# Moving a batch's key products from the first transform into the first feed-forward layer

## The chip, the cores and the metric

The kernel runs on one core of a Trainium2 chip. The metric is the device time of one execution in microseconds (us); lower is better. A core has a matrix engine (TensorE, PE in the profile, with its weight loads as PEld), VectorE (DVE), ScalarE (ACT), GpSimd (POOL), and SyncE (SP), which here issues nearly all DMAs.

## The reference, cut to what matters

Eight batches of 576 tokens, eight heads of 64 (so 512 columns), all float32. Attention of the "efficient" kind comes first, then a Fourier mix, a normalisation and two layers:

```
q_s = softmax(q over the 64 of a head)        k_s = softmax(k over the 576 tokens)
kv  = k_s^T v    (64x64 for each head)        x   = q_s kv            -> (batch, 576, 512)
u   = x + real(fft over tokens and columns of x)
un  = (u - mean) / sqrt(var + 1e-6)           (per token)
out = u + relu(un @ w1) @ w2                  (512 -> 2048 -> 512)
```

## The kernel before, in words

**Tiling.** Of each batch's 576 tokens, 512 are its own rows (four tiles of 128: `xpart(b, c, u)`), and the other 64 of two batches are gathered in a shared tile. So there are eight groups of 512 rows for the own tokens, and a ninth group (`B` = 8) for the shared ones. `attention(b)` runs stages over items: four key items (`k_load`, `k_exp`, `k_turn`, `k_times_v`: load two heads' keys and values, exponential, five transposes, ten recorded passes of matmul into `kvr`), and four query items (`q_load` to `q_times_kv`). `transform(b)` folds the tokens, runs five `block(k)` steps on PE and evacuates them on ACT into `Z` and `ZT`; `mix_own` and `mix_shared` (through `second`) finish the Fourier mix and add it to x. `norm(g)` takes the statistics, normalises and transposes x into `unT`.

**The order.** Group 0 goes through the layers plainly (`plain`): 16 `up(f)` steps of 128x512 matmuls with a relu on ACT, then 64 `part(i, f)` steps (`DOWN`). All later groups use Strassen's seven products (`up`, `down`). While PE is in group 0's layers, the other engines bring the weights into shape: `fetch(i)` loads one of 32 raw blocks of 512 KB, `convert(i)` makes floats of them (two activations on ACT, two operations on DVE, one on POOL), and `combine(layer, p)` forms the sums that Strassen needs and stores them in DRAM (`w1s`, `w2s`), from where later groups stream them. `WORDS_AT` says in which place each raw block lies; a place is used again when its block is converted (`after`). Side steps of batch 1 (attention, transform, mix, norm) are put between the 64 `part` steps by the list `gaps`.

**What sets the order.** The program's order is a priority: Tile's scheduler may let a ready instruction of later code run in a gap of its own planned time, on each engine's in-order queue. So the code has one-element operations that make later work wait: `wait_for(t, raws)` holds blocks of weights until t is there, `gate(t, raw)` does the same for other data, and `hold()` keeps the tiles q, k and v from being loaded before a given relu `f` of `up` is done (`free(f)`).

**What the change touches.** In the kernel before, batch 1's four key items are loaded at the start (`first`, lines 225 to 252, into spare space), their maxima and exponentials run in `second_keys` (lines 441 to 465) beside the folds of the first transform, and their transposes and products run as `products` between batch 0's mix and `norm(0)`:

```
one, two = front(0)
keys, products = blk.second_keys()
for step in one + keys + two + products + norm(0):
    step()
```

Eighteen conversions are in the program's 16 `up` steps (after the first four), and ten are left for the `part` steps.

Of the kernel before, what the change touches and what calls it, by code (L numbers as in the profile page):

```python
# [40 lines left out]
F32 = mybir.dt.float32  # L41
I32, U32 = mybir.dt.int32, mybir.dt.uint32
ACT = mybir.ActivationFunctionType
# [30 lines left out]

WORDS_AT = [*range(8), 8, 9, 10, *range(3, 8), 0, 1, 2, 8, 9, 10, 4, 5, 6, 7, 8, 9, 10, 11, 12, 13]
ORDER = (1, 6, 5, 7, 2, 4, 3)
# [46 lines left out]
class _Block:  # L123
    def __init__(self, ctx, tc, q, kT, v, w1, w2, ft, cd, out):
# [50 lines left out]
        self.xs, self.live, self.stream = {}, {}, {}  # L175
        self.turns = 0
        self.unused = None

# [31 lines left out]
    def first(self, fetch):  # L210

        nc, b = self.nc, 0
        at = 2 * NF * D

        def place(n):
            nonlocal at
            at += n
            return self.big[:, at - n:at]

        ks = [place(S) for _ in range(NR)]  # L220
        v = place(NC * D).rearrange("p (c n) -> p c n", n=D)
        own = [place(2 * D).rearrange("p (c n) -> p c n", n=D) for _ in range(2)]
        tail = place(D)

        k1 = self.spare(NR * S)
        flat = self.w1sb[:, NF - 2:, :].rearrange("p a n -> p (a n)")
        v1 = [self.spare(NC * P), self.spare(NC * P), place(NC * P), flat[:, 0:NC * P]]
        self.unused = None
        self.second_at = k1, [t.rearrange("p (c n) -> p c n", n=P) for t in v1]
# [17 lines left out]
        for r in range(NR):  # L247
            cols = slice(r * P, (r + 1) * P)
            t = self.second_at[1][r]
# [56 lines left out]
    def weights(self):  # L306
# [6 lines left out]
        def fetch(i):  # L313

            at = WORDS_AT[i]
            if at < 8:
                raw = self.w2sb[:, 2 * at:2 * at + 2, :].rearrange("p a n -> p (a n)")
            elif at < 11:
                raw = self.words[at - 8][:].rearrange("p a n -> p (a n)")
            else:  # L320
                raw = self.spare(2 * D)
# [95 lines left out]
    def attention(self, b, loads=None):  # L417
# [22 lines left out]

    def second_keys(self):


        nc, V = self.nc, self.nc.vector
        items = [("k", 1, r) for r in range(NR)]
        m, rec = (self.small.tile([P, NR], F32, tag=n, name=n, bufs=1) for n in ("km1", "krec1"))

        def maxima():
            self.gate(self.at_start[2][0][:, 1, :], self.second_at[0][0:1, ::S])
            for it in items:  # L450
                self.k_load(it)
                V.reduce_max(m[:, it[2]:it[2] + 1], self.live[it][0], axis=AX.X, negate=True)
            self.gate(self.xpart(0, 1, 1), m[0:1, :])

        def exps():
            for it in items:
                k, i = self.live[it][0], slice(it[2], it[2] + 1)
                nc.scalar.activation(k, k, ACT.Exp, bias=m[:, i], accum_out=rec[:, i])
                self.live[it].append(rec[:, i])

            t = self.small.tile([P, 1], F32, tag="root", name="root", bufs=1)
            nc.scalar.activation(t[:], rec[:, NR - 1:], ACT.Sqrt)
            V.tensor_scalar(out=rec[:], in0=rec[:], scalar1=ATT_EPS, scalar2=None, op0=ALU.add)
            V.reciprocal(rec[:], rec[:])
        return [maxima, exps], pipelined(items, [self.k_turn, self.k_times_v])

    def gate(self, t, raw):

        n = int(np.prod(raw.shape))
        raw, one = raw.bitcast(I32), t.bitcast(I32)[0:1, 0:n]  # L470
        if len(raw.shape) == 3:
            one = one.rearrange("p (a b) -> p a b", b=raw.shape[2])
        self.nc.vector.scalar_tensor_tensor(out=raw, in0=one, scalar=0, in1=raw, op0=ALU.bitwise_and,
                                            op1=ALU.bitwise_or)

    def k_load(self, it):
        nc, (_, b, r) = self.nc, it
        if b == 0:
            ks, v = self.at_start[:2]
            self.live[it] = [ks[r], v[:, :, r * P:(r + 1) * P]]  # L480
            return
        if b == 1:
            self.live[it] = [self.second_at[0][:, r * S:(r + 1) * S], self.second_at[1][r]]
            return
        k = self.work.tile([P, S], F32, tag="k", name="k", bufs=2)[:]
        v = self.work.tile([P, NC, P], F32, tag="v", name="v", bufs=2)
        nc.sync.dma_start(k, self.kT[b, r * P:(r + 1) * P, :])
# [24 lines left out]
    def k_turn(self, it):  # L512
# [3 lines left out]
        for c in range(4):  # L516
            nc.tensor.transpose(pt[:, c, :], k[:, c * P:(c + 1) * P], self.ident[:])
        nc.scalar.copy(ks[:, 0:4, :], pt[:])
        pt = self.turned()

# [5 lines left out]
    def k_times_v(self, it):  # L526
# [5 lines left out]
        for h in range(2):  # L532
            s = slice(64 * h, 64 * h + 64)
            to = self.kvr[b % 2][s, r, s]
            if b == 1:

                nc.scalar.mul(to, pk[s, s], rec[s, 0:1])
            else:
                nc.vector.tensor_scalar(out=to, in0=pk[s, s], scalar1=rec[s, 0:1], scalar2=None, op0=ALU.mult)

    def q_load(self, it):
# [8 lines left out]
        self.nc.sync.dma_start(q, self.q[b, tokens(c, u), :])  # L550
        self.live[it] = [q]

    def t_load(self, it):
# [85 lines left out]
    def transform(self, b):  # L639
# [36 lines left out]
        def at_first():  # L676
# [4 lines left out]

            self.wait_for(eo[1][:, NN:], [self.raws[0]])

# [34 lines left out]
    def second(self, z, zr, add):  # L718
# [13 lines left out]
        nc.scalar.copy(paired(sn[:, 0:HD]), interleaved(pm[:, HD:]))  # L732
        if self.turns == 1:

            self.gate(sn[:], self.second_at[0][0:1, ::S])
        two = self.halves()
# [16 lines left out]
    def mix_own(self, b, c):  # L753
# [3 lines left out]
        def add(lo, hi):  # L757
            for u, (f, g) in enumerate(((lo, hi), (hi, lo))):
                x = self.xpart(b, c, u)
                self.added(x, f, g)  # L760

        self.second(lambda k: Z[:, k, s], self.Zr[:, s], add)

    def norm(self, g):
# [22 lines left out]
        def normal(i):  # L787
            un = self.halves()
            x = self.xpart(g, i % 2, i // 2)
            if g == 0:  # L790
                V.tensor_scalar(out=un[:, 0:D], in0=x, scalar1=std[:, i:i + 1], scalar2=mv[:, i, 0:1], op0=ALU.mult,
                                op1=ALU.add)
                if i == 0:
                    words = self.w2sb.rearrange("p f n -> p (f n)").rearrange("p (a n) -> p a n", n=2 * D)
                    self.gate(un[:], words[0:1, 1:4, 0:2])
                if i == 1:
# [205 lines left out]
def kernel(ctx: ExitStack, tc: tile.TileContext, q, kT, v, w1, w2, ft,  # L1002
# [52 lines left out]
    one, two = front(0)  # L1055
    keys, products = blk.second_keys()
    for step in one + keys + two + products + norm(0):
        step()

    groups = [*range(B - 1), B, B - 1]  # L1060
    for order, g in enumerate(groups):
        loads = [] if g == 0 else None
        one, two = front(order + 1, loads) if order + 1 < B else (blk.later, [])
        if g == 0:
            up, down = blk.plain(0, nexts.pop(0))

            round_blocks(range(4))
            n = 2 * NF - 14
            for f in range(NF):
# [7 lines left out]
            for step in loads:  # L1077
                step()
            for i in range(3):
                fetch(2 * NF - 3 + i)  # L1080

            side = one + two + norm(1)
            gaps = [6] + [4] * (len(one) - 1) + [3] * 5 + [1] * 4 + [2] * (len(two) - 9) + [1] * 7
            at = 0
            for i in range(len(down)):
                down[i]()
                for step in rest[i // 3:i // 3 + 1] if i % 3 == 0 else []:
                    step()
                for step in combine[i * len(combine) // 60:(i + 1) * len(combine) // 60]:
                    step()  # L1090
# [63 lines left out]
```

## Time and profile before

| | |
|---|---|
| median of 3 runs | 1135.42 us (1135.22, 1135.42, 1136.85) |
| the profiled execution | 1136.85 us, span in the trace 1135.1 us |
| busy share of the span | PE 97%, PEld 81%, DVE 47%, ACT 36%, POOL 29% |
| mean granted TensorE clock | 0.993 |
| DMA | 193.79 MB, mean 171 GB/s |
| first `up` matmul of group 0 | 65.56 us from the span's start |
| first `part` matmul of group 0 | 122.15 us |
| first matmul of the next group's layers | 202.25 us |

Views of the trace give busy time per engine, and for the idle time before an instruction what ended it (the releaser). "Timeline" lines have: start in us, duration in us, engine (a trailing q is the engine's queue), source line, operation, output<-input, shape, count, and in brackets the idle time before with its releaser. "Waits" lines have: engine, tile and line of the waiting instruction, the releaser, total us, times, longest us. "Windows" lines have the stretch, its length, and for each engine busy us and the number of instructions, then the granted TensorE clock, the mean busy share of the DMA engines and GB/s.

### The profile page before, as it was taken

The page shows a single profiled execution, that of the slowest core. Times are in us where ns is not written, and L with a number is a line of the kernel's source. Part 1 is how long each engine was busy: PE and PEld are TensorE (multiplying, and loading weights), DVE is VectorE, ACT ScalarE, POOL GpSimd, SP SyncE. Part 2 cuts the span into 40 slices and gives each one's busy share as a digit, 9 for nine tenths or more (in the row PEclk, how much of TensorE's full clock was granted, in tenths as well). Part 3 has the DMA queues.
Part 4 walks back from the last instruction along what each step waited for, and adds up shares of the span by engine and source line. Part 5 has one row for each costly group of instructions (what it writes and reads, how often), then busy time and mean ns, then how long its engine had stood idle before and what let it go on. Part 6 is the DMA issues. An engine that isn't in the chain of part 4 may idle for free.

```text
span 1135.1 us, 14578 instructions
## 1 busy us (share of the span) xinstructions
PE 1096.6 (97%) x5448; PEld 916.9 (81%) x5448; DVE 533.4 (47%) x1094; ACT 404.6 (36%) x975; POOL 332.2 (29%) x304
## 2 busy tenths in 40 slices
PE   5789999999999999999999999999999999999997
PEld 4644455888888988888889888888889888888886
DVE  6675756368434724384344733592434352203201
ACT  6595523355233513371325322451334152201200
POOL 2055462235003610334024402260034213402320
PEclk9899999999999999999999999999999999999999
DMA  9557675555346534544356425552453344444451
GB/s 312 166 190 227 244 272 161 169 208 167 113 156 215 182 140 144 194 158 177 122 178 220 149 103 183 190 198 107 144 191 150 113 154 160 175 150 151 156 185 55
DMA packets 92549, 193.79 MB, mean 171 GB/s; under 512 B 23088, under 2 KB 59696, under 8 KB 85312
## 3 DMA queue, kind: packets, MB, share of 16 engines
q1 hardware_dynamic: 90680, 191.82, 49.6%
q10 hardware_dynamic: 1800, 1.05, 0.3%
q8 instruction: 43, 0.70, 0.2%
q14 instruction: 26, 0.21, 0.1%
HBM read 168.72 MB, written 28.31 MB: 174 GB/s over the span
## 4 chain that ended last, share of the span: by engine, by line
PE 83%; DVE 4%; DMA 3%; ACT 2%; issue 2%; POOL 1%; SPq 0%; POOLq 0%; ACTq 0%; DVEq 0%
PE bb L905 15%; PE bb L943 15%; PE bc L943 10%; PE ba L943 10%; PE bc L905 10%; PE ba L905 9%; PE acc L531 3%; PE acc L613 2%; PE acc L725 1%; PE acc L701 1%; PE acc L704 1%; DMA w2s<-big 1%; PE bc L844 1%; PE tr L805 1%; PE tr L581 1%
## 5 line engine op out<-in xcount | busy, mean ns | idle before, releaser
L905 PE MATMUL bb<-unT,big 128*128 128x256 f32 x768 | 187.8, 381 | 0.3 <-DVE u L873 0.3
L943 PE MATMUL bb<-big 128*128 128x256 f32 x768 | 172.1, 379 | 0.0
L943 PEld LDWEIGHTS bb<-big 128*128 128x128 f32 x768 | 145.4, 190 | 20.3
L905 PEld LDWEIGHTS bb<-unT,big 128*128 128x128 f32 x768 | 142.8, 190 | 23.5 <-DVE u L873 3.1
L354 POOL TENSOR_TENSOR big<-big 128x512 f32<-128x512 f32 (+1 forms) x38 | 46.4, 1220 | 281.4 <-ACT big L917 273.9
L905 PE MATMUL bc<-unT,big 128*128 128x256 f32 x512 | 125.6, 379 | 0.0
L905 PE MATMUL ba<-unT,big 128*128 128x256 f32 x512 | 123.6, 379 | 0.0
L917 ACT ACTIVATE big<-big 128x512 f32<-128x512 f32 x96 | 60.3, 628 | 173.8 <-DVE big L916 173.5
L943 PE MATMUL bc<-big 128*128 128x256 f32 x512 | 116.0, 379 | 0.5 <-DVE x L960 0.5
L877 DVE TENSOR_TENSOR u<-bb,s 128x512 f32<-128x512 f32 x40 | 27.6, 691 | 186.1 <-PE bb L943 128.3
L943 PE MATMUL ba<-big 128*128 128x256 f32 x512 | 114.8, 379 | 0.0
L943 PEld LDWEIGHTS bc<-big 128*128 128x128 f32 x512 | 96.1, 190 | 14.3 <-DVE x L960 0.9
L943 PEld LDWEIGHTS ba<-big 128*128 128x128 f32 x512 | 95.6, 190 | 12.1
L905 PEld LDWEIGHTS bc<-unT,big 128*128 128x128 f32 x512 | 95.1, 190 | 12.6
L905 PEld LDWEIGHTS ba<-unT,big 128*128 128x128 f32 x512 | 95.0, 190 | 11.8
L362 POOL TENSOR_TENSOR unT<-unT 128x512 f32<-128x512 f32 x8 | 14.2, 1774 | 182.9 <-DVE unT L361 182.9
L570 ACT ACTIVATE q<-q,qm 128x64 f32<-128x64 f32 x240 | 62.1, 339 | 13.8 <-DVE qm L568 13.8
L873 DVE TENSOR_TENSOR u<-bb,s 128x512 f32<-128x512 f32 x40 | 27.6, 690 | 74.3 <-PE bb L905 35.2
L955 POOL TENSOR_TENSOR x<-x,u 128x512 f32<-128x512 f32 x14 | 17.7, 1267 | 147.8 <-DVE u L877 111.2
L916 DVE TENSOR_TENSOR big<-bc,u 128x512 f32<-128x512 f32 x64 | 44.1, 689 | 25.3 <-PE bc L905 24.5
L869 ACT COPY s<-ba 128x512 f32<-128x512 f32 x40 | 23.4, 586 | 88.6 <-PE ba L905 45.5
L809 ACT COPY unT<-tr 128x512 f32<-128x512 f32 x36 | 20.7, 585 | 78.8 <-PE tr L805 78.4
(230 smaller groups left out, 1647.3 us busy)
## 6 DMA issues: line engine op xcount, KB each, us to landing
big<-w1s SPq DMA_DIRECT2D x64, 896.0 KB
big<-w2s SPq DMA_DIRECT2D x56, 1024.0 KB
big<-in_w_dram SPq DMA_DIRECT2D x20, 512.0 KB
q<-in_q_dram SPq DMA_DIRECT2D x27, 256.0 KB
k<-in_kT_dram SPq DMA_DIRECT2D x24, 288.0 KB
v<-in_v_dram SPq DMA_DIRECT2D x24, 256.0 KB
words<-in_w_dram SPq DMA_DIRECT2D x9, 512.0 KB
w2s<-big SPq DMA_DIRECT2D x8, 512.0 KB
```

What stands on the lines that cost most here:

```text
L354: e1.tensor_tensor(out=to(4), in0=at(2), in1=at(3), op=ALU.add)
L531: nc.tensor.matmul(pk, lhsT=ks[:, c, :], rhs=v[:, c, :], start=(c == 0), stop=(c == NC - 1))
L570: nc.scalar.activation(heads[:, h, :], heads[:, h, :], ACT.Exp, bias=m[:, h:h + 1])
L613: nc.tensor.matmul(px[:, r * P:(r + 1) * P], lhsT=qT[:, r, :], rhs=self.kvr[b % 2][:, r, :], start=True, stop=True)
L809: nc.scalar.copy(unT[:, u:u + 3:2, :, cols], pt[:].rearrange("p (a k) t -> p a k t", a=2))
L869: nc.scalar.copy(temp("s1"), box["ba"][:])
L873: V.tensor_tensor(out=temp("u2"), in0=box["bb"][:], in1=box["s1"][:], op=ALU.add)
L877: V.tensor_tensor(out=temp("u3"), in0=box["bb"][:], in1=box["s1"][:], op=ALU.add)
L905: nc.tensor.matmul(bank()[:, i, :], lhsT=w[:, WA_AT[m], k * P:(k + 1) * P], rhs=unT[:, B_AT[m], k, :], start=first and i == 0 and k == 0, ...
L916: V.tensor_tensor(out=hp(i), in0=bank[:], in1=u[:], op=ALU.add)
L917: nc.scalar.activation(hp(i), hp(i), ACT.Relu)
L943: nc.tensor.matmul(bank()[:, i, :], lhsT=h[p][:, A_AT[m], i * P:(i + 1) * P], rhs=w[:, p, :], start=first and i == 0 and p == 0, stop=p == ...
```

## The change

Batch 1's key items are no longer done at the start. They go back into `attention(1)` as the first four items, loaded and computed between the `part` steps of group 0. Their loads go into two k and v tiles held until relu 12, and into spare space (the place of `unT`, which is free when the last `up` step is done). In the place of the removed steps come: three junk matmuls (`warm`) behind each of the four x updates of batch 0's mix; a root that loads ACT's table at the end of the first folds; a looser hold on the weights, so that four blocks instead of one may be converted during the first transform's blocks. Twenty-four instead of eighteen conversions stand in the `up` steps, and four instead of ten among the `part` steps; the last three raw blocks get places 7, 8, 9 instead of three spare ones. The products of batch 1 are scaled by DVE instead of ACT, and batch 1's query exponentials wait for its third key's transposes (`held_back`).

```diff
-WORDS_AT = [..., 4, 5, 6, 7, 8, 9, 10, 11, 12, 13]
+WORDS_AT = [..., 4, 5, 6, 7, 8, 9, 10, 7, 8, 9]
...
-        k1 = self.spare(NR * S)
-        flat = self.w1sb[:, NF - 2:, :].rearrange("p a n -> p (a n)")
-        v1 = [self.spare(NC * P), self.spare(NC * P), place(NC * P), flat[:, 0:NC * P]]
...
-            load(self.second_at[0][:, r * S:(r + 1) * S], self.kT[1, cols, :])
-            load(t[:, 0:4, :], self.v[1, 0:512, cols].rearrange("(c p) n -> p c n", p=P))
-            load(t[:, 4, :], self.v[1, S - P:, cols])
...
-        held = {12: [("q", D, 3)] * 3, 15: [("k", S, 2)] * 2 + [("v", NC * P, 2)] * 2}
+        held = {12: [("k", S, 2)] * 2, 14: [("q", D, 3)] * 3}
...
-        if b == 1:
-            items = []
...
-    def second_keys(self):
...
-    def gate(self, t, raw):
...
+        if b == 1 and r > 1:
+            k, v = self.spare(S), self.spare(NC * P).rearrange("p (c n) -> p c n", n=P)
...
+        if it[1:] == (1, 2):
+            self.wait_for(ks[:, 0, :], [q.bitcast(I32) for q in self.held_back])
...
-            if b == 1:
-                nc.scalar.mul(to, pk[s, s], rec[s, 0:1])
-            else:
-                nc.vector.tensor_scalar(out=to, in0=pk[s, s], scalar1=rec[s, 0:1], ...)
+            nc.vector.tensor_scalar(out=self.kvr[b % 2][s, r, s], in0=pk[s, s], scalar1=rec[s, 0:1], ...)
...
-            self.wait_for(eo[1][:, NN:], [self.raws[0]])
+            t = self.small.tile([P, 1], F32, tag="root", name="root", bufs=1)
+            V.tensor_scalar(out=t[:], in0=eo[1][:, NN:NN + 1], scalar1=0.0, scalar2=None, op0=ALU.mult)
+            nc.scalar.activation(t[:], t[:], ACT.Sqrt)
+            self.wait_for(eo[1][:, NN:], [self.raws[i] for i in range(4)])
...
                 self.added(x, f, g)
+                if b == 0:
+                    self.warm(x[:, 0:HD], 3)
...
-    for step in one + keys + two + products + norm(0):
+    for step in one + two + norm(0):
...
-            n = 2 * NF - 14
+            n = 2 * NF - 8
...
-            for i in range(3):
-                fetch(2 * NF - 3 + i)
...
-            gaps = [6] + [4] * (len(one) - 1) + [3] * 5 + [1] * 4 + [2] * (len(two) - 9) + [1] * 7
+            gaps = [2] + [2] * 4 + [8] + [2] * (len(one) - 6) + [3] * 5 + [1] * 4 + [2] * (len(two) - 9) + [1] * 7
+            other = rest + combine
...
-                for step in rest[i // 3:i // 3 + 1] if i % 3 == 0 else []:
-                    step()
-                for step in combine[i * len(combine) // 60:(i + 1) * len(combine) // 60]:
+                for step in other[i * len(other) // 60:(i + 1) * len(other) // 60]:
```

More of the change, by code (lines that the diff above doesn't have):

```diff
@@ L72 @@
 WB_AT = {1: 0, 2: 1, 3: 2, 4: 6, 5: 4, 6: 5, 7: 3}
-WORDS_AT = [*range(8), 8, 9, 10, *range(3, 8), 0, 1, 2, 8, 9, 10, 4, 5, 6, 7, 8, 9, 10, 11, 12, 13]
+WORDS_AT = [*range(8), 8, 9, 10, *range(3, 8), 0, 1, 2, 8, 9, 10, 4, 5, 6, 7, 8, 9, 10, 7, 8, 9]
 ORDER = (1, 6, 5, 7, 2, 4, 3)
@@ L176, in __init__ @@
         self.turns = 0
+        self.held_back = []
         self.unused = None
@@ L223, in first @@
         tail = place(D)
-        k1 = self.spare(NR * S)
-        flat = self.w1sb[:, NF - 2:, :].rearrange("p a n -> p (a n)")
-        v1 = [self.spare(NC * P), self.spare(NC * P), place(NC * P), flat[:, 0:NC * P]]
-        self.unused = None
-        self.second_at = k1, [t.rearrange("p (c n) -> p c n", n=P) for t in v1]
         load = nc.sync.dma_start
@@ L246, in first @@
         self.tables()
-        for r in range(NR):
-            cols = slice(r * P, (r + 1) * P)
-            t = self.second_at[1][r]
-            load(self.second_at[0][:, r * S:(r + 1) * S], self.kT[1, cols, :])
-            load(t[:, 0:4, :], self.v[1, 0:512, cols].rearrange("(c p) n -> p c n", p=P))
-            load(t[:, 4, :], self.v[1, S - P:, cols])
         for i in range(11):
@@ L317, in fetch @@
                 raw = self.w2sb[:, 2 * at:2 * at + 2, :].rearrange("p a n -> p (a n)")
-            elif at < 11:
+            else:
                 raw = self.words[at - 8][:].rearrange("p a n -> p (a n)")
-            else:
-                raw = self.spare(2 * D)
             raw = raw.bitcast(I32)
@@ L439, in attention @@
         return steps
-    def second_keys(self):
[L444 to L465, printed above, removed]
-    def gate(self, t, raw):
[L469 to L474, printed above, removed]
     def k_load(self, it):
@@ L481, in k_load @@
             return
-        if b == 1:
[L483 to L486, printed above, removed]
+        if b == 1 and r > 1:
+            k, v = self.spare(S), self.spare(NC * P).rearrange("p (c n) -> p c n", n=P)
+        else:
+            k = self.work.tile([P, S], F32, tag="k", name="k", bufs=2)[:]
+            v = self.work.tile([P, NC, P], F32, tag="v", name="v", bufs=2)
         nc.sync.dma_start(k, self.kT[b, r * P:(r + 1) * P, :])
@@ L533, in k_times_v @@
             s = slice(64 * h, 64 * h + 64)
[L534 to L539, printed above, removed]
+            nc.vector.tensor_scalar(out=self.kvr[b % 2][s, r, s], in0=pk[s, s], scalar1=rec[s, 0:1], scalar2=None,
+                                    op0=ALU.mult)
     def q_load(self, it):
@@ L551, in q_load @@
         self.live[it] = [q]
+        if b == 1:
+            self.held_back.append(q)
     def t_load(self, it):
@@ L732, in second @@
         nc.scalar.copy(paired(sn[:, 0:HD]), interleaved(pm[:, HD:]))
-        if self.turns == 1:
-            self.gate(sn[:], self.second_at[0][0:1, ::S])
         two = self.halves()
@@ L792, in normal @@
                                 op1=ALU.add)
-                if i == 0:
-                    words = self.w2sb.rearrange("p f n -> p (f n)").rearrange("p (a n) -> p a n", n=2 * D)
-                    self.gate(un[:], words[0:1, 1:4, 0:2])
                 if i == 1:
@@ L1055 @@
     one, two = front(0)
-    keys, products = blk.second_keys()
-    for step in one + keys + two + products + norm(0):
+    for step in one + two + norm(0):
         step()
```

## The prediction

> **What bounds the kernel now.** I read the page first (busy shares, slices), then the waits of PE, then timelines of the two places where PE is not full.
>
> ```profile
> PE 1096.6 (97%) x5448; PEld 916.9 (81%) x5448; DVE 533.4 (47%) x1094; ACT 404.6 (36%) x975; POOL 332.2 (29%) x304
> PE   5789999999999999999999999999999999999997
> PEclk9899999999999999999999999999999999999999
> ```
>
> PE is the bound from the third slice (57 us) on. The slices before it have spare PE time, and the change takes work out of there and puts it where PE is full. How full is told by the waits of PE between the first `up` matmul of group 0 (65.56 us) and the first matmul of the next group (202.25 us):
>
> ```profile
> PE acc L701 <- ACT ZT L712: 2.7, 1, 2.7
> PE tr L805 <- ACT eo L799: 1.5, 2, 0.9
> PE ba L835 <- ACT unT L809: 1.1, 1, 1.1
> PE acc L613 <- ACT qT L588: 0.9, 1, 0.9
> ```
>
> That is 6.2 us of waits in 136.7 us, so whatever PE work is added there costs nearly its length. Now the stretch before it, timeline from 50 us, where the key products (L517, L521, L531, L537) stand between batch 0's mix and its norm:
>
> ```profile
> 52.01 1.28 DVE L774 BATCH_NORM_STATS2 st<-x 128x6 f32<-128x512 f32 x2
> 53.42 1.27 DVE L774 BATCH_NORM_STATS2 st<-x 128x6 f32<-128x512 f32 x2
> 55.83 0.63 ACT L537 ACTIVATE kvr<-acc,krec 64x64 f32<-64x64 f32 x2 [1.47 <-PE acc L531]
> 57.38 0.30 ACT L778 ACTIVATE std<-mv,eps 128x2 f32<-128x2 f32 x1
> 57.71 0.17 DVE L779 RECIPROCAL std<-std 128x2 f32<-128x2 f32 x1 [3.02 <-ACT std L778]
> 59.28 1.00 DVE L791 TENSOR_SCALAR eo<-x,std,mv 128x512 f32<-128x512 f32 x2
> 59.84 1.38 PE L531 MATMUL acc<-big,ks 128*128 128x128 f32 x10 [0.79 <-ACT ks L518]
> 61.05 1.04 PE L805 MATMUL tr<-ident,eo 128*128 128x128 f32 x8
> 62.66 1.08 ACT L809 COPY unT<-tr 128x512 f32<-128x512 f32 x2
> ```
>
> The first statistics are done at 53.5, but the root (L778) comes at 57.38, because ACT's queue holds the key copies and scalings that wait for PE; DVE idles 3.02 us for it. The normalised x is done at 60.28, and its transposes then stand behind the fourth key product on PE. So the key products delay the first `up` step here.
>
> **The change part by part.** *Start of group 0's layers.* Without the products the root runs right behind the first pair of statistics (53.5 + 0.3), and the reciprocal behind the second pair, which ends at 54.7 and 0.2 later with its aggregate: 54.9 instead of 57.71, or 2.8 earlier. From the reciprocal to the last normalised tile before took 60.28 - 57.71 = 2.6, so 57.5. The first transposes need only the first tile (55.7) and no longer wait for a product; copies of 0.59 follow, the last of four transposes at about 57.6 to 58.2, its copy to 58.9, `up` at 59.0: 6.5 earlier. Against it: four conversions may now run during the transform's blocks. Each takes 0.65 + 0.68 on ACT and twice 0.69 on DVE (L342, L347, L343, L344). ACT was busy 2.70 of 5 us in 40 to 45 and 2.17 in 45 to 50, so there is room for the 5.3 us, but one of these operations in front of a Z copy, one in front of an add and one in front of a root cost up to 0.7 each. I take 1.0 in all (bounds 0 and 4): `up` starts 5.5 earlier (2.5 to 6.5). The maxima taken out (L452, 2.73 us at 29.34) saved nothing: they end at 32.07, and the next fold needs an x copy that ends at 32.01. The twelve `warm` matmuls lie behind the x updates and end before the first transposes.
>
> The table of the root was loaded at 37.15 in 1.28 us (L462), in an ACT gap. It can still load there, since the load itself waits for nothing, or beside the blocks; I count 0.3, inside the 1.0. "ScalarE: Activation LUTs", What ACT_TABLE_LOAD costs, in the Trainium skill gives such a switch 2.66 us with a drain behind the load; the row shows the root directly behind its 1.28 us, and with the page's figure beside the blocks the forecast would be some 1.4 us higher.
>
> *The key items on PE.* Batch 2's, run inside Strassen's layers at full clock, show their price (timeline of PE, 210 to 245 us):
>
> ```profile
> 214.41 0.60 PE L517 MATMUL tr<-ident,k 128*128 128x128 f32 x4
> 214.85 0.27 PE L521 MATMUL tr<-ident,k 128*128 128x128 f32 x1
> 217.55 1.28 PE L531 MATMUL acc<-v,ks 128*128 128x128 f32 x10
> ```
>
> By start to next start that is 214.41 to 214.96 = 0.55 and 217.55 to 218.66 = 1.11, so 1.66 for one item, 6.6 for four. All of it now lies among the `part` steps, where PE is full: +6.6.
>
> *Waits of the key items.* `k_exp`, `k_turn`, `k_times_v` now follow each other by two `part` steps, 1.7 us, on PE's in-order queue; what is queued behind a late one is all the rest of the layer. The keys themselves are in time: relu 12 falls at about 60 + 13 x 3.43 + 0.6 = 105, and two keys need 3 us to land; the two in the spare place are issued when `up` ends (some 116.5) and turned about 8 us later. But ACT's ks copy (0.58) and DVE (5.00 of 5 us busy in 125 to 130) must answer within 1.7 us. Bounds: 0, and 3.6 (four times the 0.9 by which PE waited for qT in this stretch). Batch 2's own four keys waited 1.1 once and 1.2 in two, so I take 1.5, nearer to these.
>
> *Loads, conversions, stores.* Keys and values of batch 1 (2.36 MB) go from the start, where they pushed the raw weights back, to 105 to 120 us; the DMA engines were 0.32 busy in 110 to 120, which covers them. They stand on SP in front of the queries, whose exponentials moreover wait (`held_back`, four one-element operations on DVE) for the third key's ks copy, about 125 us; that costs nothing while the first query is turned at step 18, some 137 us, and one query's exponentials take 2.0 us on ACT (L570). Twenty-four conversions in 55 us of `up` need 24 x 1.38 = 33 us of DVE and 32 + 16 x 0.6 = 42 us of ACT: covered. The `part` steps lose six conversions (8.3 us of DVE, 7.7 of POOL) and get the keys (four times 0.74 + 0.30 + 0.58 = 1.6 us of DVE, the scaling among it). Zero; without that cover a conversion behind time would hold a `part` at its own 1.3 us.
>
> *The stall at 180 us.*
>
> ```profile
> 178.93 0.77 ACT L507 ACTIVATE k<-k,km 128x576 f32<-128x576 f32 x1 [4.92 <-DVE km L505]
> 180.28 0.76 PE L701 MATMUL acc<-ft,eo 128*128 128x144 f32 x4 [2.75 <-ACT ZT L712]
> 182.80 1.06 SPq L392 DMA_DIRECT2D w2s<-big  x2
> 180.00:185.00 5.00, 4.72 (x13) 2.66 (x14) 1.92 (x5) 1.64 (x12) 1.63 (x2) 0.66 0.73 224
> ```
>
> Z copies of batch 1 stand on ACT behind an exponential of batch 2's second key, whose load stands on SP behind w2s stores and whose maximum stands on DVE behind the sums of w2. PE waits 2.75 us and then runs at a granted clock of 0.66: 181.67 to 184.77 for four passes of 0.43, some 1.8 us more. I keep this 4.5 us as it is (bounds: gone, or as now).
>
> "TensorE: Matmul & The Clock Gate", Part 1, in the Trainium skill has the clock halved after an idle window of about 3.4 us; here 2.75 us of wait were enough. Taken as a threshold, the rule would price this stall at 2.75 us, and the faster rival would lie 1.8 us nearer to the forecast.
>
> Sum: -5.5 + 6.6 + 1.5 = +2.6. The profiled execution took 1136.85 us (span 1135.1 and 1.75 around it), so 1139.4 against it; but it is the highest of three, and I put the difference on the median, 1135.4: **1138.0**. The first `up` step starts cold in both (granted clock 0.68 in 65.5 to 70), so no difference is taken from that.
>
> **The rivals.** *Faster: the combine chain gets a head start.* `combine` can begin when `up` ends (POOL L354 waited 12.3 us for L279, until 120.03), which is 5.5 us earlier, while batch 1's Z copies stay where they are in time, since the key items fill that gain. If the last w2s stores move from 182.8 to before 177, the key of batch 2 is loaded early and the 4.5 us stall goes, with it the 0.9 us wait for qT; with key waits of 0.5: -5.5 + 6.6 + 0.5 - 5.4 = -3.8, 1131.6. It decides from the point where ACT's Z copies wait under 0.5 us. For it: six conversions less on POOL and DVE behind 120 us. Against it: the w2 sums stand later in the program among the steps than before, and DVE and ACT have the keys first.
>
> *Slower still: the start moves little.* The conversions let loose in the first transform take ACT and DVE in front of the mix, and `up` starts only 2.5 us earlier: -2.5 + 6.6 + 1.5 = +5.6, 1141.0. For it: ACT put a conversion (42.33) in front of the second block's Z copy already before. Against: about 5 of 10 us of ACT are free there.
>
> *No change:* 6.5 us gained, no wait of the keys: +0.1, 1135.5.
>
> **How the numbers follow.** A change of 0.2%, 2.3 us, is about what a measurement of this kernel can tell from none. The forecast has 0.42 (0.30 slower by more than that, 0.12 within); the faster rival 0.29 (0.25 faster, 0.04 within); the small start 0.16, all slower; no change 0.13 (0.08 within, 0.03 faster, 0.02 slower). Faster 0.28, same 0.24, slower 0.48. The forecast's own range is 1135.5 to 1141.6 (start 4 to 6.5 earlier, waits 0 to 3.6). The whole range reaches over the rivals, 1130.1 (the faster one with a start 6.5 earlier and no waits: -5.3) to 1143.1 (start 2.5 earlier, waits 3.6: +7.7), leaving out what lies past these ends and new waits that no row shows.
>
> **What would show it.** Right: the first `up` matmul near 60 us, the root behind its statistics; key pieces of 0.55 and 1.11 us on PE between 117 and 140; the first matmul of the next group 2 to 3 us behind 202.25, and all later groups shifted by the same. Wrong: `up` at 63 or later; PE waits for ks or k above 4 us; no wait of PE for ZT near 180 and a next group that starts before 200; or a difference that arises after the next group has started, which nothing here foresees.

## The result and the profile after

| | before | changed |
|---|---|---|
| median, four runs of each on one chip | 1135.32 us (1134.85 to 1136.85) | 1140.72 us (1138.83 to 1142.04) |
| ratio | | 1.0044, interval 1.0025 to 1.0062 |
| ratio on a second chip (run `after_again`) | 1137.18 us (31 runs, 1131.59 to 1140.68) | 1139.48 us, 1.0025, interval 1.0007 to 1.0043 |
| profiled execution, span | 1136.85 us, 1135.1 | 1142.04 us, 1140.2 |
| first `up` matmul | 65.56 | 60.98 |
| first `part` matmul | 122.15 | 117.5 |
| first matmul of the next group, in the timeline of PE | 202.09 | 202.91 |
| first matmul of `down` in the seventh Strassen group | 982.7 | 987.9 |

By the two ratios the change makes the kernel slower by 2.8 and 5.0 us; the forecast was 2.6. (The start of the next group before is 202.09 us in the timeline; the 202.25 given earlier is in no view.) The page's first lines, its slices and its clock show nothing of how:

```profile
PE 1101.9 (97%) x5472; PEld 922.9 (81%) x5472; DVE 541.6 (47%) x1110; ACT 402.9 (35%) x967; POOL 332.3 (29%) x302
PE   5899899999999999999999999999999999999997
PEclk9999999999999999999999999999999999999999
```

The start of group 0 is where the forecast was made first. Timeline from 50 us:

```profile
52.09 1.28 DVE L727 BATCH_NORM_STATS2 st<-x 128x6 f32<-128x512 f32 x2
53.37 0.66 DVE L330 TENSOR_SCALAR big<-bc 128x512 int32<-128x512 int32 x1
54.15 0.30 ACT L731 ACTIVATE std<-mv,eps 128x2 f32<-128x2 f32 x1 [0.28 <-DVE mv L728]
55.92 0.17 DVE L732 RECIPROCAL std<-std 128x2 f32<-128x2 f32 x1
59.24 0.63 PE L755 MATMUL tr<-ident,eo 128*128 128x128 f32 x4 [0.80 <-DVE big L250]
60.98 2.04 PE L785 MATMUL ba<-unT,big 128*128 128x512 f32 x2 [1.11 <-ACT unT L759]
```

The root (L731) stands 0.28 us behind its statistics, as forecast, and no key product is in front of the transposes. One conversion (L330) was let in between the statistics of the second and third tile, and the second reciprocal came at 55.92 instead of the 54.9 of the working: one of the costs for which 1.0 was set aside.

Now PE's waits from the first `up` matmul to the next group. They hold one new line, and the forecast's four old ones are down to the wait for unT:

```profile
PE acc L484 <- ACT ks L468: 3.8, 1, 3.8
PE ba L785 <- ACT unT L759: 1.1, 1, 1.1
PE tr L755 <- ACT unT L759: 0.2, 1, 0.2
PE acc L564 <- DVE kvr L487: 0.2, 1, 0.2
```

The 3.8 us are explained by the timeline of the other engines in front of 128.09:

```profile
125.07 0.93 DVE L343 TENSOR_TENSOR big<-big 128x256 f32<-128x256 f32 x1 [2.63 <-POOL big L341]
125.92 0.74 DVE L455 TENSOR_REDUCE km<-spare 128x1 f32<-128x576 f32 x1
126.69 0.78 ACT L457 ACTIVATE spare<-spare,km 128x576 f32<-128x576 f32 x1 [8.37 <-DVE km L455]
127.47 0.56 ACT L468 COPY ks<-tr 128x512 f32<-128x512 f32 x1
128.09 1.75 PE L484 MATMUL acc<-v,ks 128*128 128x128 f32 x10 [3.84 <-ACT ks L468]
129.63 1.06 PE L467 MATMUL tr<-ident,k 128*128 128x128 f32 x4
130.69 1.85 PE L794 MATMUL bb<-big 128*128 128x512 f32 x2
```

PE had turned the first key at 121.82. ACT's copy of it (L468) stood in ACT's queue behind the third key's exponential (L457), that one waited for its maximum (L455), and the maximum stood on DVE behind a sum of `combine` (L343) that waited for POOL. So the first key waited for the third, whose load had been issued only at 118.78, and the third waited for sums of weights. That it was the sums and not the load itself is read from the chain that ended last: it goes from a w1s store (118.30, 4.51 us) over POOL's sums (123.63 and 124.36) to the maximum.

The stall at 180 us is gone. First from the kernel before, SP's issue of batch 2's second key with the stores ahead of it, and PE's first step of the transform's blocks:

```profile
170.64 2.42 SPq L392 DMA_DIRECT2D w2s<-big  x2
174.64 0.79 SPq L487 DMA_DIRECT2D k<-in_kT_dram  x1
170.01 0.66 PE L701 MATMUL acc<-ft,eo 128*128 128x144 f32 x4
```

And from the changed kernel, SP's issues of both keys, ACT's first exponential and first Z copy, and the same step of PE:

```profile
164.54 0.44 SPq L437 DMA_DIRECT2D k<-in_kT_dram  x1
166.78 0.37 SPq L437 DMA_DIRECT2D k<-in_kT_dram  x1
175.63 0.78 ACT L457 ACTIVATE k<-k,km 128x576 f32<-128x576 f32 x1 [12.44 <-DVE km L455]
177.52 0.37 ACT L661 COPY Z<-acc 128x256 f32<-128x256 f32 x1
175.29 0.66 PE L655 MATMUL acc<-ft,eo 128*128 128x144 f32 x4
```

Before, the second key's load stood behind two w2s stores and its exponential in front of the Z copies, at 178.93. Now the load is 7.9 us earlier, PE's blocks begin 5.3 us later, and both exponentials are done (at 177.4) when the first Z copy is due. Windows of the changed kernel (PE is full where before had a wait; the other two belong to the ks wait):

```profile
126.00:128.00 2.00, 0.00 (x0) 0.00 (x0) 1.36 (x5) 1.31 (x3) 0.00 (x0) 1.00 1.05 406
130.00:132.00 2.00, 2.00 (x7) 1.37 (x6) 1.92 (x5) 1.23 (x3) 0.68 (x1) 0.50 0.01 5
175.00:185.00 10.00, 10.00 (x44) 6.57 (x43) 6.01 (x14) 4.45 (x19) 4.56 (x6) 1.00 0.68 223
```

Up to the next group the two executions differ by 0.8 us only. The rest of the difference in the profiled run arises later, first in the next group. The chain that ended last (start, length, what):

```profile
248.20 0.64 PE tr L532 x4
248.85 5.63 DMA q<-in_q_dram
...
256.49 1.49 DVE q L526
...
258.01 0.66 PE tr L532 x4
```

A query of batch 2 is loaded when the transposes of another have freed its place (248.84), lands 5.63 us later, and after its normalising PE has waited 2.39 us for it. With the half clock behind this wait (0.66 in 258 to 260, 0.50 in 260 to 262) the distance from the next group's start to the one after it is 126.7 us instead of 123.8. Before, the queries of that batch went to PE at other times, with one wait of 0.94 at 256.29. Another 1.4 us arise two groups on (123.5 us instead of 122.0 from one group's start to the next), where PE waits 2.03 us for a query at 502.28.

### The profile page after: what moved, and what is told of

Same layout as the page of the kernel before. It is cut to its first block, busy times and chain, and to the rows that moved or that the text cites. A ratio compares the mean times of both kernels' runs of the same rounds, so it can differ in the third digit from the quotient of the medians.

```text
span 1140.2 us, 14646 instructions
## 1 busy us (share of the span) xinstructions
PE 1101.9 (97%) x5472; PEld 922.9 (81%) x5472; DVE 541.6 (47%) x1110; ACT 402.9 (35%) x967; POOL 332.3 (29%) x302
## 4 chain that ended last, share of the span: by engine, by line
PE 86%; DVE 5%; DMA 3%; ACT 3%; issue 1%; POOL 1%; SPq 0%; ACTq 0%; POOLq 0%; DVEq 0%
PE bb L893 15%; PE bb L855 14%; PE bc L893 10%; PE ba L893 10%; PE bc L855 10%; PE ba L855 9%; PE acc L484 3%; PE acc L564 2%; PE bc L794 2%; PE acc L655 2%; PE acc L658 2%; PE acc L679 1%; PE tr L532 1%; PE tr L755 1%; PE tr L467 1%
## 5 line engine op out<-in xcount | busy, mean ns | idle before, releaser
L349 POOL TENSOR_TENSOR unT<-unT 128x512 f32<-128x512 f32 x8 | 14.2, 1775 | 183.0 <-DVE unT L348 183.0
L661 ACT COPY Z<-acc 128x256 f32<-128x256 f32 (+1 forms) x32 | 12.0, 375 | 107.1 <-PE acc L658 107.1
```

## The experiments

Each ratio is to the kernel before on the same chip. Two executions of one kernel can differ by more than what is looked for here, so the ratios carry the verdicts, and the profiles the places.

**The two kernels again.** Unaltered.

> The changed kernel once more, unaltered, for a second trace. If the loss of 5 us has the three places that its first trace shows (0.8 us by the start of the next group, 2.9 in that group's up layer, 1.4 in the up layer two groups on), they stand in the second trace as well, each within 0.5 us, and the time is 1138 to 1142. If the two later places are chance of one execution (loads that landed late), they are gone or elsewhere in this trace, and the time is nearer to 1138.

Measured: 1.0025, interval 1.0007 to 1.0043, span 1136.5. The ks wait was there again (3.7 us), the stall at 180 was not, `up` began at 60.8 and the next group at 202.5. The query wait in the next group was half as long, and the clock stayed at 1.00 behind it:

```profile
PE tr L532 <- DVE q L526: 1.2, 1, 1.2
```

From the next group's start to the `down` of the seventh took 785.0 us in the first profile and 781.5 in this one. So 3.5 us of the first profile's loss differ from one execution to the next: 2.1 in the next group, where the wait was half as long and the clock stayed full, and the 1.4 two groups on, which are gone.

> The kernel before, unaltered, for a second trace. Theory: its stall near 180 us (ACT's Z copies behind the second exponential of batch 2) is a matter of the order in ACT's queue, so it is there again, with 2 to 3.5 us of wait and slow clock behind it, and from the first part to the next group it takes 79 to 81 us as in the first trace (79.9). Rival: it came from one late load; then the wait is under 1 us here and the distance is near 75.

Measured: one execution of 1139.1 us, span 1137.3. The stall was there again (3.1 us for ZT, granted clock 0.75 in 175 to 185), so it lies in the order on ACT and not in one execution. First `up` 64.4, next group 203.8 (81.5 us after the first `part`, a little over the 79 to 81 expected), and 780.7 from there to the same `down` (780.6 in the first profile). Against this execution the second one of the change is 3.6 us earlier at `up` and 1.3 earlier at the next group, where the first pair of profiles had 4.6 earlier and 0.8 later. So a term read from one pair of profiles holds to a microsecond or two, no better.

**The third key held.** In `k_exp` of the changed kernel:

```diff
+        if it[1] == 1 and it[2] > 1:
+            self.wait_for(self.kss[it[2] % 2][:, 0, :], [k.bitcast(I32)])
```

> The changed kernel with one wait more: the exponentials of batch 1's third and fourth key wait for the ks copies of the first and second, so that ACT has the copy first; nothing is loaded earlier. Theory A (the loss at 124 us is ACT's order: a copy that was ready stood behind an exponential whose data were not): PE's wait of 3.84 us for ks falls below 1 us, the slow clock behind it goes, and the next group starts 4 to 6 us earlier, at 197 to 199; time some 1135 to 1137. Rival B (the keys' loads are late, whatever the order): the wait only moves to the third key's transposes on PE, and the next group still starts at 202 to 203; time as changed, 1139 to 1141.

Measured: 1.0003, interval 0.9989 to 1.0018. PE's waits between 100 and 200 us:

```profile
PE acc L566 <- DVE kvr L489: 1.6, 1, 1.6
PE bc L787 <- ACT big L789: 1.3, 1, 1.3
PE tr L534 <- DVE qrec L526: 0.8, 1, 0.8
PE acc L486 <- ACT ks L470: 0.6, 2, 0.3
```

The ks wait falls from 3.8 to 0.6 with the clock loss behind it, and the next group starts at 200.3, later than the 197 to 199 expected. It was 202.9. Of the 5.6 us of wait and lost clock (worked out below), 0.6 stay and 2.4 come back as waits for DVE (the last key's scaling and a query's sum). The difference to the unaltered change is 1.0025 - 1.0003 = 0.22%, 2.5 us. The intervals overlap, but the runs of the two, taken together on one chip, hardly do: nine of ten of `order_only` (median 1136.73) are under the lowest of `after_again` (1137.66, median 1139.48). So the order that makes the ks wait is shown to be that part of the loss.

**The third key loaded earlier.** Its keys go into the tile of Z instead of the spare place:

```diff
-            k, v = self.spare(S), ...
+            k = self.spare(S) if r == 3 else self.work.tile([P, KT * HD], F32, tag="Z", ...)[:, 0:S]
```

> The changed kernel with the third key of batch 1 in the idle space of Z, so that its load needn't wait for the end of up; its values and the fourth key stay in the spare space. Theory A (ACT's order): the third key's exponential is done before the first copy, so PE's wait for ks falls below 1 us, as in the other kernel; next group at 197 to 199, time 1135 to 1137. Rival B (loads): the fourth key and the third's values are as late as before, so 2 us or more of PE waits stay between 120 and 145 us, and the time stays above 1138.

Measured: 0.9999, interval 0.9981 to 1.0016. No ks wait is left; the kvr wait of 1.6 and one of 0.9 for qT are. Another way to the same end, and the same time within its interval. The next group starts at 201.75, not at the 197 to 199 expected; behind the waits for qT and kvr the clock halved (see the end).

**The scaling back on ACT.** `order_only`, with batch 1's products scaled by ACT as before the change:

```diff
+            if b == 1:
+                nc.scalar.mul(to, pk[s, s], rec[s, 0:1])
```

> The changed kernel with the wait that puts the ks copies first, and with batch 1's products scaled by ACT as in the kernel before instead of DVE. Theory A (with the order mended, DVE's queue is what is late next: the fourth key's scaling stood behind query work and PE waited 1.6 us for it): that wait goes, the next group starts 1 to 2.5 us before the 200.3 of the version with the order alone, and the time falls to 0.1 to 0.2% below the kernel before. Rival (PE's later steps wait anyway for the queries): a wait of the same size for q or qT takes its place, and the next group starts at 200 to 201.

Measured: 0.9997, interval 0.9983 to 1.0011, the same as `order_only`. The kvr wait went, and in its place came

```profile
PE acc L486 <- ACT ks L470: 2.0, 1, 2.0
```

with the next group at 200.3 again, as the rival said: a wait of the same size took its place, here in front of the second key's product (130.42) instead of the query product that needed the last key's scaling (146.81).

**The stall taken out of the kernel before.** Batch 2's first two key loads wait for its last Z row:

```diff
+        if b == 2 and r < 2:
+            nc.vector.tensor_copy(k[0:1, 0:1], self.Zr[0:1, 0:1])
```

> The kernel before with the loads of batch 2's first two keys held until the last Z copy of batch 1's transform, so that no exponential stands in front of those copies on ACT. Theory A: the stall at 180 us is that order alone; PE's 2.75 us wait for ZT and the half clock behind it go, and the next group starts 4 to 4.5 us earlier, near 198; time 1130.5 to 1132. Rival B: the stall is due to w2's sums and stores on DVE and SP, which delay the Z stage by themselves: a wait of 2 us or more of PE stays near 180, and the time stays at 1134 to 1136.

Measured: 0.9982, interval 0.9967 to 0.9996, median 1134.27 us, so 2 us faster and not the 1130.5 to 1132 expected. No wait for ZT; the first `part` to the next group takes 75.1 us instead of 79.9. Some 2.5 us are given back in the next group (126.3 us to the one after it, instead of 123.8), where a query's transposes wait 2.2 us.

**Both kernels without the key items.** Batch 1's keys are not turned or multiplied: before keeps their loads, changed leaves them out too (and its list `gaps` begins with 18, so that the queries don't come earlier). Of each diff the lines that matter:

```diff
-    keys, products = blk.second_keys()
-    for step in one + keys + two + products + norm(0):
+    for step in one + [root] + two + norm(0):
```
```diff
+        if b == 1:
+            items = []
```

> The kernel before without batch 1's key maxima, exponentials, transposes and products (their loads stay, and a root keeps its place): batch 1's output is not the reference's. It prices the key items where they stood. Theory: up starts 4.5 to 5.5 us earlier (60 to 61 us instead of 65.6), and since nothing is added later, 4 to 5 us are left at the next group if the 180 us stall stays; time 0.4% below the kernel before. Rival (the keys were hidden in idle time): up starts at 64 or later and the time is the same.

> The changed kernel without batch 1's key items, loads included: batch 1's output is not the reference's. It prices the key items where they now stand. Theory: they cost 6.6 us of PE and 5.7 us of wait and slow clock, so the next group starts some 12 us earlier, near 190 to 191, and the time is 0.8 to 1.0% below the changed kernel, unless the queries, freed from the keys, run into the stall at 180 us again (then 4.5 less). Rival (PE has slack beside the keys): the next group starts at 195 or later without any such stall.

Measured: 0.9949 (0.9932 to 0.9966) and 0.9994 (0.9980 to 1.0009). In the old place the keys cost 0.51%, 5.8 us, and it arises at the start (`up` at 59.1 instead of 65.56, 6.4 us). In the new place they seem to cost 1.0025 - 0.9994 = 0.31%, 3.5 us, less than their own 6.6 us on PE and far less than the 0.8 to 1.0% expected. And the change without keys is 0.45% slower than before without keys, 5.1 us. In the profiles 1.9 us of this stand at the first `up` already (61.08 against 59.14), for which the forecast had 1.0; the rest is in no step of it. PE's waits and DVE's timeline of `after_nokeys` show where:

```profile
PE acc L657 <- DVE eo L627: 4.4, 1, 4.4
PE acc L657 <- ACT ZT L668: 2.2, 1, 2.2
```
```profile
156.85 0.43 DVE L348 TENSOR_TENSOR big<-big 128x256 f32<-128x256 f32 x1 [13.41 <-DMA w2s<-big]
159.41 1.21 DVE L605 TENSOR_TENSOR eo<-x 128x512 f32<-128x512 f32 x1
161.95 1.75 DVE L605 TENSOR_TENSOR eo<-x 128x512 f32<-128x512 f32 x1
```

Batch 1's folds (L605 on) stand on DVE behind the third and fourth pair of sums of w2 (L348, L350), and the third waits 13.41 us for the place that a w2s store still reads. So the next group starts at 203.5, far from the 190 to 191 expected and no earlier than with the keys. In before without keys only one such sum stands in front, and the folds begin at 157.16 and end at 164.6 instead of 171.27.

**The folds in front of those sums.** In `combine`, for w2, in four kernels (`self.fold` is batch 1's folded tile; in the two of the kernel before, these steps also come a little later in the list):

```diff
+            if p in (2, 3):
+                self.wait_for(self.fold, [w[:, p, :].bitcast(I32)])
             self.b_side(quarter, place, nc.vector, nc.gpsimd, nc.gpsimd)
```

> The changed kernel without batch 1's key items (their loads, exponentials, transposes and products are left out, so the output is not the reference's), as in after_nokeys, and now VectorE does the third and fourth pair of sums of w2 behind batch 1's folds: before each of them stands a one-element operation that takes the last fold's tile. In after_nokeys VectorE stood 13.41 us in front of the third pair of sums (L348, waiting for the store of w2s until 156.85), the folds came behind it and ended at 171.27, and PE waited 4.4 us for eo and 2.2 us for ZT. Theory (the place of the sums in VectorE's queue is what the rest of the change costs): the folds end some 10 us earlier, by about 160, both waits go, the next group starts at about 197 instead of 203.5, and the ratio falls from 0.9994 to about 0.994, that of before without keys. Rival (the folds are late for another reason, such as late query items): they end after 167, at least 4 us of PE's waits stay, and the ratio stays within 0.2% of 0.9994. Second rival (later sums give it back): the next group starts earlier, but PE waits for streams of w2s or for key items behind it, and the ratio is above 0.997.

Measured: 0.9938, interval 0.9923 to 0.9954; span 1127.0. PE's waits from 160 to 195 us, then POOL's timeline:

```profile
PE tr L761 <- ACT eo L755: 1.5, 2, 0.9
PE acc L661 <- ACT ZT L672: 1.3, 1, 1.3
PE acc L661 <- DVE eo L631: 0.3, 1, 0.3
```
```profile
155.92 0.73 POOL L349 TENSOR_TENSOR big<-big 128x256 f32<-128x256 f32 x1 [12.90 <-DMA w2s<-big]
157.31 0.72 POOL L349 TENSOR_TENSOR big<-big 128x256 f32<-128x256 f32 x1 [0.66 <-DMA w2s<-big]
157.99 2.48 POOL L607 TENSOR_TENSOR eo<-x 128x512 f32<-128x512 f32 x2
```

The 6.6 us at the transform are down to 1.6, the next group starts at 194.6 instead of 203.5, and more than the 5.1 us is gone (0.9938 against 0.9949). It is shown that the sums' place in the queues costs the change 0.56%, 6.4 us, when it has no keys. That this is the whole difference to before without keys isn't shown: that kernel has a wait of its own for ZT (2.6 us, with slow clock behind it) and was not run with the sums held. One number was missed: the folds ended at 166.3, not by 160, since POOL has folds and sums too, and its own sum (L349) was not held; DVE then stood 9.38 us for POOL.

> The changed kernel with all key items, the third key held as in order_only, and the third and fourth pair of sums of w2 held behind batch 1's folds. order_only had ratio 1.0003, the next group at 200.3, and no wait of PE above 0.2 us between 150 and 200. Theory (with the keys on PE the late folds are already covered by PE's own work, so moving them earlier gains nothing): the folds end by about 165 instead of 172.1, PE is as full as it was, the next group starts between 199.5 and 201, and the ratio is 0.999 to 1.002. Rival (late folds also push the rest back on VectorE, such as the query scalings and the norm): the next group starts below 198.5 and the ratio is below 0.998.

Measured: 1.0002, interval 0.9993 to 1.0011, as `order_only`. With the keys on PE the late folds cost nothing that the interval (0.1%, 1 us) would show; the reading is that the key products fill the time in which PE would have waited for them. The next group started later in this profile than expected (204.0), since `up` itself began at 63.0 and waits of 1.6 (kvr), 1.2 (ZT) and 0.9 were there; from there to the following group it took 122.0 us, so the total is unchanged. The price of the keys is now 1.0002 - 0.9938 = 0.64%, 7.3 us: their 6.6 us and a little waiting. With the third key held and the sums not held, the same price reads 1.0003 - 0.9994 = 0.09%, 1 us: the other 6 are covered by the wait for the folds that PE has without keys. The 3.5 us above are this 1 us and the 2.5 of the ks wait.

> The kernel before with only this: the third and fourth pair of sums of w2 held behind batch 1's folds. Before has VectorE idle for 10.39 us in front of one sum (L361, released at 160.81) with the folds behind it (161.15 to 169.5), and PE waits 2.75 us for a ZT copy at 180 and runs at a granted clock of 0.66 behind it, which is 4.5 us. Theory: the folds end before 162, the Z copies stand on ACT ahead of batch 2's second key, the wait for ZT and the slow clock behind it go, the next group starts at 197 to 199 instead of 202.1, ratio 0.996 to 0.998. Rival (the stall comes from the loads of batch 2's keys and its place on ACT alone): the wait stays between 2 and 4 us, and the ratio is 0.999 to 1.001. Other side (the later sums bring w2s stores, and with them batch 2's key loads, some 8 us later, and the layers of group 1 wait for them): above 1.001.

Measured: 0.9975, interval 0.9962 to 0.9989. The ratio is as expected; the reason is half so. The wait for ZT did not go: 

```profile
PE acc L705 <- ACT ZT L716: 1.6, 1, 1.6
```

A key's exponential still stood in front of the Z copies (176.07), but with 1.6 instead of 2.75 us the granted clock stayed at 1.00. The folds ended at 166.7, again behind POOL, and the next group began at 199.5, just past the 197 to 199 expected.

> before_held (the kernel before, with batch 2's first two key loads held until its Z is done; ratio 0.9982, next group at 195.3, of which 2.5 us were given back in group 1) and the third and fourth pair of sums of w2 held behind batch 1's folds. Theory: PE waited only 1.5 us (eo of the norm) between 150 and 200 there, so the earlier folds can give at most about 1 us more: next group at 194 to 195.5, group 1 gives the same 2 to 3 us back, ratio 0.997 to 0.9985. Rival: the sums of w2 and the held keys now both come later, group 1 waits for them by 2 us more, and the ratio is 0.9995 to 1.001.

Measured: 0.9964, interval 0.9947 to 0.9981, median 1131.34 us; next group at 195.9, 124.4 us to the one after it. That is better than the 0.997 to 0.9985 expected: the group after gives back 0.6 us and not 2 to 3. PE's only wait between 150 and 200 us:

```profile
PE tr L811 <- ACT eo L805: 1.5, 2, 0.9
```

This version, the old place of the keys with two orders mended, is faster than the kernel before by 4 us, and the change was slower than that kernel. Its interval overlaps those of its two parts, so that the parts add up is not shown.

## Why the prediction was right, and where it was not

The sign and the size hold: +2.6 us forecast, +5.0 and +2.8 measured. The sum up to the next group does not, and that the size comes out is in good part luck, since several errors cancel. The forecast's own sign of being right, a next group 2 to 3 us later and all groups behind it shifted by the same, did not come: it was 0.8 later in the first pair of profiles and 1.3 earlier in the second. Terms by the first two profiles, in us:

| step of the forecast | forecast | measured | from |
|---|---|---|---|
| Start of group 0's layers | -5.5 | -4.6 | 65.56 to 60.98 |
| The key items on PE | +6.6 | +6.6 | 0.54 and 1.12 where undisturbed: the third item's turn, 134.36 to 134.90, and the second's product, 133.24 to 134.36 |
| Waits of the key items | +1.5 | +5.6 | 3.84 of wait, and at half clock behind it 0.94 on two pieces of key items and 0.83 on two `part` matmuls |
| The stall at 180 us | 0 | -4.5 | PE full, granted clock 1.00 |
| waits for eo (1.5) and qT (0.9) | 0 | -2.4 | no longer among PE's waits |
| to the next group's start | +2.6 | +0.7 | read: 202.91 - 202.09 = +0.8 |
| groups after it | 0 | +4.4 and +0.8 | 785.0 and 781.5 against 780.6 and 780.7 |

*Start.* Within its bounds, and by the mechanism named: root behind its statistics, no product in front of the transposes. `before_nokeys`, where only the key items are left out, began `up` at 59.14, which is the 59.0 of the working. The change began 1.8 us later, and 1.5 of it stand already at the first statistics (52.09 against 50.54), so the 1.0 set aside for conversions and table was too small, by these two executions. The root's table was loaded beside the blocks (L635, 40.79, 1.28 us), in front of the first ZT copies and not in a gap, and the root came at 42.09, directly behind. "ScalarE: Activation LUTs", What ACT_TABLE_LOAD costs, in the Trainium skill adds 1.38 us of drain to such a load; here the activation started 1.30 us after the load did, so the trace does not agree with the addition.

*Waits of the key items* is the term that was mis-sized. The forecast looked at each item's own answer time within two steps, and took its bound from waits of 0.9 and 1.2 elsewhere. It said that the third key would come late (issued when `up` ends) and did not ask what stands behind it: on ACT the first key's copy. That is the step that failed: 1.5 (at most 3.6) was forecast, 5.6 measured. Its own sign of error, a wait for ks above 4 us, was just missed (3.8), while the cost with the clock was above the upper bound of 3.6. `order_only` takes this wait away and 2.5 us of the loss with it.

*The stall at 180 us* was kept and went. It was the faster rival's gain, and it came by half of the rival's mechanism: batch 2's second key was loaded 7.9 us earlier (166.78 instead of 174.64). But the w2s stores had not moved before 177, as the rival had it: SP issued two at 175.56 and two more from 181.78, now behind the key's load. And PE's blocks began 5.3 us later, which gave the exponentials time as well. Which of the two was needed, no run tells apart. Had the ks wait stayed at its 1.5, the terms would give -4.6 + 6.6 + 1.5 - 4.5 - 2.4 = -3.4 at the next group, near that rival's -3.8. With the ks wait taken out, though, the change only became equal to before (1.0003), so that rival's total is not reached either.

*Loads, conversions, stores: zero.* Right for the change as it is, and only since the keys cover it: without them the order of the sums costs 6.4 us (0.9994 to 0.9938). The forecast had seen that the w2 sums stand later among the steps, but asked only whether there is enough engine time, not what stands behind them in DVE's and POOL's queues.

*Later groups.* A difference that arises there was listed as what would make the prediction wrong, and part of it does. In both profiles of the change a query of batch 2 is late for PE in the next group, by 2.39 and 1.2 us; the chain above shows why for the first, and no run moved these loads alone. With the same change in them, `early_third` and `folds_order` have 780.0 and 779.1 in the same stretch, `order_only` 781.7 and `order_act` 785.0, so it is not a fixed price. What the later groups cost on average stays open.

## What to carry to other kernels

Work moved onto the bounding engine costs its length only where nothing else would have held that engine: find the second floor (here folds behind sums behind a store) by leaving the moved work out, in both kernels. When a late item is put into an in-order queue, list what is queued behind it on every engine that it passes; here the first key waited for the third, and the third for sums of weights. A one-element operation that makes the blocking work wait for the urgent work was worth more than moving the keys.

## What the runs showed of the hardware

The granted clock fell to half behind waits of PE, and the length of one wait did not decide it. From the first `up` step on, every wait from 2.19 us up was followed by two or more microseconds at 0.50 to 0.66: 2.19 (`before_held`), 2.25 (`after_nokeys`), 2.39 (the change), 2.53 (`order_act`, at 498.14) and the longer ones up to 4.41 us. Below that both are found. Four windows behind a wait, in this order: 1.63 us at 146.78 in `early_third` (0.9 us of another wait had ended at 144.2), 1.97 at 252.09 in `folds_before`, 1.99 at 130.42 in `order_act`, 2.03 at 502.28 in the change:

```profile
146.00:150.00 4.00, 3.22 (x9) 2.22 (x10) 1.57 (x5) 1.17 (x2) 0.72 (x1) 0.57 1.02 407
252.00:256.00 4.00, 3.91 (x16) 3.47 (x17) 3.45 (x5) 1.84 (x4) 3.63 (x3) 0.61 0.56 217
130.00:134.00 4.00, 3.58 (x19) 2.34 (x19) 4.00 (x10) 3.35 (x8) 2.37 (x3) 1.00 0.60 237
502.00:506.00 4.00, 3.72 (x24) 3.46 (x25) 3.86 (x8) 2.50 (x9) 3.92 (x3) 1.00 0.57 201
```

The shorter two cost the clock, the longer two did not. "TensorE: Matmul & The Clock Gate", Part 1, in the Trainium skill puts the idle window at about 3.4 us; in these runs much shorter waits were enough at times, and between 1.6 and 2.1 us the length does not tell the cases apart. A drop is why 1.2 us more of waiting in the next group of the change came with 1.7 us of lost clock: (1 - 0.66) x 2 + (1 - 0.50) x 2 in 258 to 262 us.

The same fold on DVE (two inputs of 128x512) took 0.69 us at 143.18 in `folds_nokeys`, with POOL idle, and 1.75 us at 161.95 in `after_nokeys`, beside POOL's own folds.
